# Efficient attention followed by a leaky-ReLU feed-forward layer: one row of q moved from TensorE transposes into a DMA transpose, and three warm-up products left out

## The chip, the cores and the metric

The kernel runs on one core of a Trainium2 chip. The core has five engines with instruction streams of their own: TensorE (PE in the profile; its weight loads are listed as PEld), VectorE (DVE), ScalarE (ACT), GpSimd (POOL) and SyncE (SP), which here only issues DMAs. They share one on-chip memory (SBUF) and one accumulation memory for TensorE (PSUM), and they wait for one another by semaphores. The metric is the device time of one execution in microseconds (us). Lower is better.

## The reference

Inputs are q, k and v of shape (8, 8, 576, 64): batches, heads, positions, head width. The matrices w_in (512 x 2048) and w_out (2048 x 512) follow.

```python
q_s = softmax(q, axis=-1)          # over the 64 of a head
k_s = softmax(k, axis=2)           # over the 576 positions
kv  = einsum('bhsd,bhse->bhde', k_s, v)
x   = einsum('bhsd,bhde->bhse', q_s, kv)      # -> (4608 tokens, 512)
h   = x @ w_in
out = maximum(0.01 * h, h) @ w_out            # (4608, 512), float32
```

Both softmaxes subtract the maximum first and add 1e-9 to the sum.

## The kernel before

**Tiling.** A batch's tensors lie in SBUF as 128 partitions x 4 x 9 x 64 (`HL`, `R`, `D`): a partition holds nine "rows" r of four heads, the other four heads lie in the other 64 partitions. For each batch the kernel forms exp(k), casts v, and multiplies them into kv (`kv`, L333, products of line L325; `kv_pair`, L398, for batch 0). `kd_make` (L341) divides by k's sums. For q it takes the maximum (L229), subtracts it (L288), takes the exponential (`q_exp`, L295), sums (`q_sum`, L302) and multiplies by the reciprocal (`q_norm`, L309). The normalised q has to stand with d on the partitions before TensorE can multiply it with kv. `cross` (L448, products L461) does that product; the result `po` is copied into `xT`, the transposed input of the feed-forward layer.

**How q is transposed.** Batch 0 goes through TensorE: `q_turn_first` (L264) for rows 0 to 3 and `q_transpose` (L425, products L429) for the rest, with a copy from PSUM by `q_keep` (L441, L444 on ScalarE and L446 on VectorE) into the tile `qT`. Batches 2 and later go through a DMA transpose on SP's queue, `q_turn` (L532). Batch 1 goes through three DMA transposes, `turn_next` (L540), from its exponentials `qe` into the tile `X1` (the trace calls it X): seven blocks of 128 columns for the head pair 0 of rows 0 to 6, seven for the head pair 1, and four for rows 7 and 8. `q_cols` (L209) lays batch 1's exponentials out so that each of the three is contiguous.

**Token tiles and order.** The feed-forward layer runs over nine tiles of 512 tokens. A batch has 576, so tile 0 is rows 0 to 7 of batch 0, and tile 1 begins with row 8 of batch 0 and continues with rows 0 to 6 of batch 1. For each tile `layer1` (L547) makes 16 products of the hidden layer, `leaky` (L556, ScalarE) writes them as `gj`, and `layer2` (L568) accumulates the output in PSUM, from which `store` (L560) copies and writes it. Every engine executes its instructions in the order in which the code issues them. The order is written out by hand: `at(t, u, ...)` hangs a step on a point of tile t, and `run(t, u)` issues it there, between products of the layers. In tile 0 the points 32 and later lie between the products of layer 2: at 44.5 comes `kv(1)` and `kd_make(1)`, at 45 `q_transpose(0, 8, 1)` with its copy on ScalarE, and at 46 `attend_next` (L522). This makes the whole xT of tile 1: for each head pair a `cross` of row 8 of batch 0 and one of rows 0 to 6 of batch 1 into the same PSUM banks, and four copies (L530), two on ScalarE and two on VectorE. Four products of layer 2 follow, and then tile 1 begins.

**SP's queue around it.** `next_loads`, at point 32, issues in this order: the first and the second `turn_next`, then the loads of k (batch 2), q's last rows (batch 1), and q and v (batch 2). SP waits at each transpose until the exponentials that it reads are normalised.

**The start.** Before any data is there, TensorE executes idle products of a zero tile: `wake(n, ...)` (L355, products L357) issues one product of n columns for each n; in float32 each is two loads and two products in the trace. `wake(TT, TT, TT, 256)` (L601) comes first, then `wake_on` (L361), a product that waits for the first maxima of q (`nmax`, L238), and shorter idle products between the steps of k's maximum of batch 0 (`k_max_pe` L366, `k_all_dve` L376, `k_all_pe` L380, `k_sub_ps` L390). The w_in matrix comes in eight DMAs from POOL's queue (L126).

**Tiles in memory.** `qe` comes from a pool of two buffers, taken in turn by batches 0, 1, 2 and so on. `X1` is a tile of its own; `qT` of batch 0 and `qX` of batches 2 and later come from a pool of two.

Of the kernel before, what the change touches and what calls it, by code (L numbers as in the profile page):

```python
# [9 lines left out]
BF16 = mybir.dt.bfloat16  # L10
# [9 lines left out]
L = 64  # L20
R = 9
HL = 4
# [3 lines left out]
def kernel(  # L26
# [9 lines left out]
    nc = tc.nc  # L36
# [3 lines left out]
    B, H, S, D = q.shape  # L40
# [6 lines left out]
    P = 128  # L47
    NB = C // P
    NF = F // P
    TT = 512  # L50
# [4 lines left out]
    const_pool = ctx.enter_context(tc.tile_pool(name="const", bufs=1))  # L55
# [4 lines left out]
    qe_pool = ctx.enter_context(tc.tile_pool(name="qe", bufs=2))  # L60
    mx_pool = ctx.enter_context(tc.tile_pool(name="mx", bufs=1))
    small_pool = ctx.enter_context(tc.tile_pool(name="small", bufs=3))
    qT_pool = ctx.enter_context(tc.tile_pool(name="qT", bufs=2))
# [11 lines left out]
    def load(src, b, name, cuts, t=None):  # L75
        t = raw(name) if t is None else t
        flat = src[b].rearrange("h s d -> (h s d)").rearrange(
            "(hl p r d) -> p hl r d", hl=HL, p=P, r=R
        )
        for hs, rs in cuts:  # L80
            nc.sync.dma_start(  # L81
                out=t[:, hs, rs].rearrange("p h r d -> p h (r d)"),
                in_=flat[:, hs, rs].rearrange("p h r d -> p h (r d)"),
            )
        return t

    ALLH, ALLR = slice(0, HL), slice(0, R)
    RA, RB = slice(0, 4), slice(4, R)
    R1, R2, R3 = slice(4, 6), slice(6, 8), slice(8, R)
    R7, RE = slice(0, 7), slice(7, R)  # L90
    st = [{} for _ in range(B)]
# [19 lines left out]
    xT = xT_pool.tile([P, NB, T], BF16)  # L111


    vb2 = [const_pool.tile([P, R, 2, 2, D + 2], BF16, name=f"vb{i}") for i in range(2)]
    kd0 = const_pool.tile([P, 2, 2, 2, D], BF16)
    kd2 = [const_pool.tile([P, 2, 2, D], BF16, name=f"kd{i}") for i in range(2)]
# [92 lines left out]
    def q_cols(b, rs, hs):  # L209
        if b != 1:  # L210
            return st[b]["qe"][:, rs, hs]
        flat = st[b]["qe"].rearrange("p r h d -> p (r h d)")
        cut = R7.stop * 2 * D
        i = 2 if rs.start else hs.start // 2
        return flat[:, i * cut : (i + 1) * cut if i < 2 else R * HL * D].rearrange(
            "p (r h d) -> p r h d", h=hs.stop - hs.start, d=D
        )

    def q_begin(b):
        st[b]["qe"] = qe_pool.tile([P, R, HL, D], BF16, name="qe")  # L220
        if b == 1:
            st[b]["X1"] = const_pool.tile([P, 2 * R, P], BF16, name="X1")
        if b == 0:
            st[b]["qT"] = qT_pool.tile([P, NB, R, L], BF16, name="qT", tag="qT")

    def q_max(b, rs, hs=ALLH):
        n, m = rs.stop - rs.start, hs.stop - hs.start
        st[b]["qmax", rs.start, hs.start] = o = small_pool.tile([P, HL, n], FP32, name="qmax")[:, 0:m]
        nc.vector.tensor_reduce(out=o, in_=st[b]["q"][:, hs, rs], axis=AX.X, op=ALU.max)  # L229
# [76 lines left out]
        st[b]["qrec", rs.start, hs.start] = qrec = small_pool.tile([P, n, HL], FP32, name="qrec")[:, :, 0:m]  # L306
        nc.vector.reciprocal(out=qrec, in_=qsum)

    def q_norm(b, rs, hs=ALLH):  # L309
        n, m = rs.stop - rs.start, hs.stop - hs.start  # L310
        qes = q_cols(b, rs, hs)
        nc.vector.tensor_tensor(  # L312
            out=qes,
            in0=qes,
            in1=st[b]["qrec", rs.start, hs.start].unsqueeze(3).to_broadcast([P, n, m, D]),
            op=ALU.mult,
        )
# [37 lines left out]
    def wake(*cols):  # L355
        for n in cols:
            nc.tensor.matmul(  # L357
                wake_ps[:, 0:n], lhsT=zero, rhs=zero[:, 0:1].to_broadcast([P, n]), start=True, stop=True
            )
# [65 lines left out]
    def q_transpose(b, r0, n, pool=psB_pool, tag=BANK_TAG):  # L425
        ps = pool.tile([P, NB, n, L], BF16, name="psum_qt", tag=tag)
        for rr in range(n):
            for gg in range(2):
                nc.tensor.matmul(  # L429
                    ps[:, gg::2, rr],  # L430
                    lhsT=st[b]["qe"][:, r0 + rr, 2 * gg : 2 * gg + 2].rearrange(
                        "p h d -> p (h d)"
                    ),
                    rhs=ident,
                    is_transpose=True,
                    start=(rr == 0 and gg == 0),
                    stop=(rr == n - 1 and gg == 1),
                )
        st[b]["ps", r0] = ps

    def q_keep(eng, b, r0, n, gs=slice(0, 4)):  # L441
        o, i = st[b]["qT"][:, gs, r0 : r0 + n], st[b]["ps", r0][:, gs]
        if eng is nc.scalar:
            eng.copy(out=o, in_=i)  # L444
        else:
            eng.tensor_copy(out=o, in_=i)  # L446

    def cross(b, gg, outs, rows):  # L448
        for hp in range(2):
            for hh in range(2):  # L450
                half = slice(hp * D, (hp + 1) * D)
                ls = slice(hh * L, (hh + 1) * L)
                if b == 1 and rows.start == R7.stop:
                    rhs = st[b]["X1"][:, 2 * R7.stop :].rearrange("c (r g) l -> c g r l", g=2)[:, gg, :, ls]
                elif b == 1:
                    rhs = st[b]["X1"][:, gg * R7.stop : (gg + 1) * R7.stop, ls]
                elif "qX" in st[b]:
                    rhs = st[b]["qX"].rearrange("c (r g) (h l) -> c g h r l", g=2, h=2)[:, gg, hh, rows]
                else:
                    rhs = st[b]["qT"][:, 2 * hh + gg, rows]  # L460
                nc.tensor.matmul(  # L461
                    outs[hp][hh * D : (hh + 1) * D].rearrange("p (r l) -> p r l", l=L),
                    lhsT=kd0[half, gg, hh, hp] if b == 0 else kd2[b % 2][half, gg, hh],
                    rhs=rhs[half],
                    start=True,
                    stop=True,
                )
# [63 lines left out]

    def q_turn(b, rs=ALLR):  # L532
        if rs.start == 0:
            st[b]["qX"] = qT_pool.tile([P, R * 2, P], BF16, name="qX", tag="qT")
        nc.sync.dma_start_transpose(
            out=st[b]["qX"][:, 2 * rs.start : 2 * rs.stop],
            in_=st[b]["qe"][:, rs].rearrange("p r h d -> p (r h d)"),
        )

    def turn_next(cols, blocks):  # L540
        nc.sync.dma_start_transpose(
            out=st[1]["X1"][:, blocks], in_=st[1]["qe"].rearrange("p r h d -> p (r h d)")[:, cols]
        )

    def layer1(j, ph, c0, n, part=slice(0, 4), first=True, last=True):
# [33 lines left out]
    def at(t, u, *fns):  # L579
        while t > 0 and u >= 32:  # L580
            t, u = t + 1, u - 32
        hooks.setdefault((t, u), []).extend(fns)
# [15 lines left out]


    HA, HB = slice(0, 1), slice(1, 2)  # L600
    wake(TT, TT, TT, 256)  # L601
    nc.gpsimd.tensor_copy(out=gate[:, 0:1], in_=st[0]["k"][:, HL - 1, R - 1, D - 1 : D])
    load_w_in(0)
    k_begin(0)
# [66 lines left out]
        load(v, 1, "v_raw", [(H0, ALLR), (H1, ALLR)], t)  # L671

    def next_loads():
        turn_next(slice(0, 7 * 2 * D), slice(0, 7))
        turn_next(slice(7 * 2 * D, 14 * 2 * D), slice(7, 14))
        st[2]["k"] = load(k, 2, "k_raw", [(H0, ALLR), (H1, ALLR)])
        load(q, 1, "q_raw", [(ALLH, RE)], st[1]["q"])
        st[2]["q"] = load(q, 2, "q_raw", [(ALLH, ALLR)])
        st[2]["v"] = load(v, 2, "v_raw", [(ALLH, ALLR)])
# [11 lines left out]
    at(0, 32, next_loads)  # L691
    at(0, 32, lambda: v_cast(nc.scalar, 1, 1), lambda: k_exp(1, H1))
    at(0, 44.5, lambda: kv(1), lambda: kd_make(1))
    at(0, 45, lambda: q_transpose(0, 8, 1), lambda: q_keep(nc.scalar, 0, 8, 1))
    at(0, 46, attend_next)
    at(1, 8, lambda: q_exp(1, RE))

# [3 lines left out]
    def plan2():  # L701
        b = 2
        at(1, 0, lambda: k_begin(b), lambda: q_begin(b), lambda: k_tree(b, H0), lambda: k_tree(b, H1))
        at(1, 2, lambda: q_max(1, RE), lambda: q_sub(nc.gpsimd, 1, RE))
        at(1, 3, lambda: q_max(b, XR[0]), lambda: q_sub(nc.gpsimd, b, XR[0]))
        at(1, 3, lambda: k_allmax(b), lambda: k_sub(nc.vector, b, H0), lambda: k_sub(nc.vector, b, H1))
        at(1, 6, lambda: q_max(b, XR[1]), lambda: q_sub(nc.gpsimd, b, XR[1]))
        at(1, 13, lambda: q_exp(b, XR[0]), lambda: q_sum(b, XR[0]), lambda: q_norm(b, XR[0]))
        at(1, 13, lambda: v_cast(nc.gpsimd, b, 0), lambda: v_cast(nc.gpsimd, b, 1))
        at(1, 14, lambda: q_sum(1, RE), lambda: q_norm(1, RE))  # L710
        at(1, 15, lambda: k_exp(b, ALLH), lambda: q_turn(b, XR[0]))
        at(1, 15, lambda: turn_next(slice(7 * HL * D, R * HL * D), slice(14, 18)))
        at(1, 16, lambda: q_exp(b, XR[1]), lambda: q_sum(b, XR[1]), lambda: q_norm(b, XR[1]))
        at(1, 17, lambda: q_turn(b, XR[1]))
        at(1, 17, lambda: load_all(4))
        at(1, 23, lambda: kv(b))
        at(1, 24, lambda: kd_make(b))
        at(1, 27, lambda: attend_all(b, (XR[0],)), lambda: attend_all(1, (RE,)))
# [28 lines left out]
    for t in range(3, B - 1):  # L747
        b = t + 1
# [33 lines left out]
    def end_act(j, ph, half):  # L782
# [11 lines left out]
        lambda: q_sub(nc.vector, 0, R3),  # L794
        lambda: q_exp(0, R3),
        lambda: q_sum(0, R3),
        lambda: q_norm(0, R3),
    )
    x1 = (
        lambda: attend(0, (1,), RA),  # L800
# [100 lines left out]
```

## Time and profile before

| | |
|---|---|
| median of 3 runs | 282.1 us (281.68 to 282.16) |
| the profiled execution | 283.07 us |
| its span, first to last instruction | 281.3 us |
| PE busy, share of the span | 272.2 us, 97% |
| DVE, ACT | 159.7 and 159.9 us, 57% each |
| POOL | 49.3 us, 18% |
| q10 and q1 (DMAs issued by engines), q0 (issued by POOL) | 41.9 MB and 4.2 MB |
| q8 and q14 (instructions) | 15 and 7 packets |

The profile is one execution, a little longer than the runs without a profile. A line of a timeline gives the start in us from the span's start, the busy time in us, the engine, the line of the kernel and its operation, what is written and what is read, the shapes and the number of instructions; in brackets stand the idle time of the engine before it and what ended that. "issue" means that nothing the profile shows was waited for. A waits line gives the total, the number and the longest. The chain is followed back from the last instruction to what released each step. In the DMA view a queue has packets, MB, and its share of the time of 16 DMA engines.

### The profile page before, as it was taken

How to read it: one execution, taken by the hardware profiler on the slowest of the kernel's cores; microseconds unless marked ns; L12 is line 12 of the kernel's file. 1: busy time of each engine (PE TensorE's matmuls, PEld its weight loads, DVE VectorE, ACT ScalarE, POOL GpSimd, SP SyncE). 2: the span in 40 equal slices, each digit the busy share in tenths (PEclk: the TensorE clock that was granted, in tenths of full speed). 3: DMA queues.
4: the chain of work that ended last, by engine and by line, in shares of the span. 5: the costliest groups of instructions: out<-in, count | busy, mean ns of one | idle time of the engine just before them, and what ended most of it. 6: DMA issues, size and time to landing. Idle time of an engine off the chain costs nothing.

```text
span 281.3 us, 4853 instructions
## 1 busy us (share of the span) xinstructions
PE 272.2 (97%) x1929; PEld 133.4 (47%) x1956; DVE 159.7 (57%) x227; ACT 159.9 (57%) x283; POOL 49.3 (18%) x54
## 2 busy tenths in 40 slices
PE   8899997999999999999999999999999999999994
PEld 3478644444444454444444544454444444444443
DVE  3986895999999949966885497634610000000011
ACT  4977563685389276755586448643844364146400
POOL 2947380159003002100400050000000000000000
PEclk9999999999999999999999999999999999999999
DMA  7999997999893499089409930333033200330033
GB/s 251 326 209 323 247 235 187 400 320 357 229 396 116 53 329 359 4 223 398 120 0 259 391 90 2 84 77 69 7 86 75 64 11 2 74 75 0 2 75 75
DMA packets 39606, 46.38 MB, mean 165 GB/s; under 512 B 18464, under 2 KB 22816, under 8 KB 39584
## 3 DMA queue, kind: packets, MB, share of 16 engines
q1 hardware_dynamic: 36064, 41.75, 48.9%
q0 software_dynamic: 3360, 4.20, 8.5%
q8 instruction: 15, 0.25, 0.4%
q10 hardware_dynamic: 160, 0.13, 0.2%
q14 instruction: 7, 0.06, 0.1%
HBM read 36.70 MB, written 9.44 MB: 164 GB/s over the span
## 4 chain that ended last, share of the span: by engine, by line
PE 84%; DMA 10%; POOL 2%; issue 1%; ACT 1%; SPq 0%; DVE 0%; ACTq 0%
PE ph L547 41%; PE pout L568 40%; DMA v_raw<-in_v_dram 4%; DMA w_in_sb<-in_moe_w_in_dram 3%; DMA k_raw<-in_k_dram 2%; DMA X<-qe 2%; PE po L461 1%; POOL w_in_sb L126 1%; PE pokv L325 1%; PE pkv L325 1%; SPq L81 0%; ACT gj L556 0%; POOL vb L206 0%; POOL qe L257 0%; ACT ke L194 0%
## 5 line engine op out<-in xcount | busy, mean ns | idle before, releaser
L568 PE MATMUL pout<-w_out_sb,gj 128*128 128x512 bf16 (+2 forms) x574 | 126.4, 373 | 1.2 <-issue 0.3
L547 PE MATMUL ph<-xT,w_in_sb 128*128 128x512 bf16 (+1 forms) x631 | 126.2, 357 | 0.6
L556 ACT ACTIVATE gj<-ph 128x512 bf16<-128x512 f32 x144 | 82.2, 601 | 26.5 <-PE ph L547 25.6
L547 PEld LDWEIGHTS <-w_in_sb 128*128 128x128 bf16 x640 | 62.4, 98 | 62.2 <-DMA w_in_sb<-in_moe_w_in_dram 0.4
L568 PEld LDWEIGHTS <-gj 128*128 128x128 bf16 x592 | 56.5, 98 | 65.3 <-issue 0.2
L562 ACT COPY out_sb<-pout 128x512 f32<-128x512 f32 (+1 forms) x29 | 16.8, 581 | 68.0 <-PE pout L568 40.3
L562 DVE COPY out_sb<-pout 128x512 f32<-128x512 f32 (+1 forms) x8 | 4.8, 636 | 70.8 <-PE pout L568 70.8
L206 POOL CAST vb<-v_raw 128x1152 bf16<-128x1152 f32 x13 | 20.3, 1589 | 84.2 <-DMA v_raw<-in_v_dram 84.2
L305 DVE TENSOR_REDUCE qsum<-qe 128x36 f32<-128x2304 bf16 (+5 forms) x13 | 20.0, 1542 | 10.3 <-ACT qe L296 10.1
L194 ACT ACTIVATE ke<-k_raw 128x1152 bf16<-128x1152 f32 (+2 forms) x12 | 17.8, 1481 | 9.3 <-DVE k_raw L186 9.1
L312 DVE TENSOR_TENSOR qe<-qe,qrec 128x2304 bf16<-128x2304 bf16 (+5 forms) x13 | 22.4, 1726 | 0.4
L229 DVE TENSOR_REDUCE qmax<-q_raw 128x36 f32<-128x2304 f32 (+5 forms) x13 | 20.0, 1537 | 0.8 <-DMA q_raw<-in_q_dram 0.8
L296 ACT ACTIVATE qe<-q_raw 128x2304 bf16<-128x2304 f32 (+5 forms) x13 | 17.1, 1316 | 4.3 <-POOL q_raw L288 3.3
L186 DVE TENSOR_TENSOR k_raw<-k_raw,kall 128x1152 f32<-128x1152 f32 (+1 forms) x9 | 17.3, 1940 | 0.3
L288 POOL TENSOR_TENSOR q_raw<-q_raw,qmax 128x512 f32<-128x512 f32 (+3 forms) x7 | 11.8, 1681 | 21.4 <-DVE qmax L229 19.6
L153 DVE TENSOR_TENSOR t<-t 128x256 f32<-128x256 f32 (+2 forms) x22 | 15.0, 682 | 0.7
L484 ACT CAST xT<-po 128x448 bf16<-128x448 f32 (+3 forms) x34 | 14.4, 516 | 1.1 <-PE po L461 1.1
L288 DVE TENSOR_TENSOR q_raw<-q_raw,qmax 128x2304 f32<-128x2304 f32 (+1 forms) x6 | 13.2, 2202 | 0.3
L345 DVE RECIPROCAL krec<-pokv 128x2 f32<-128x2 f32 x8 | 1.3, 166 | 20.9 <-PE pokv L461 20.9
L153 DVE TENSOR_TENSOR t<-k_raw 128x512 f32<-128x512 f32 (+1 forms) x11 | 12.1, 1103 | 1.3 <-DMA k_raw<-in_k_dram 1.2
L357 PE MATMUL pout<-zero 128*128 128x512 f32 (+3 forms) x18 | 8.9, 616 | 1.0 <-POOL zero L100 1.0
L325 PEld LDWEIGHTS <-ke 64*64 64x64 bf16 x504 | 6.0, 107 | 3.4 <-issue 3.0
(68 smaller groups left out, 106.8 us busy)
## 6 DMA issues: line engine op xcount, KB each, us to landing
out_dram<-out_sb SPq DMA_DIRECT2D x70, 128.0 KB, 2.6
q_raw<-in_q_dram SPq DMA_DIRECT2D x6, 1152.0 KB, 9.3
v_raw<-in_v_dram SPq DMA_DIRECT2D x6, 1152.0 KB, 11.7
k_raw<-in_k_dram SPq DMA_DIRECT2D x5, 1152.0 KB, 6.5
k_raw<-in_k_dram SPq DMA_DIRECT2D x6, 576.0 KB, 6.1
v_raw<-in_v_dram SPq DMA_DIRECT2D x4, 576.0 KB, 7.6
w_in_sb<-in_moe_w_in_dram POOLq DMA_DIRECT2D x8, 256.0 KB, 7.2
w_out_sb<-in_moe_w_out_dram POOLq DMA_DIRECT2D x6, 256.0 KB, 9.4
```

Source lines behind the costliest of these rows:

```text
L153: nc.vector.tensor_tensor(out=o, in0=i0, in1=i1, op=ALU.max)
L186: eng.tensor_tensor(out=ks, in0=ks, in1=st[b]["kall"][:, hs].unsqueeze(2).to_broadcast([P, n, R, D]), op=ALU.subtract,)
L194: nc.scalar.activation(out=st[b]["ke"][:, :, hs].rearrange("p r h d -> p h r d"), in_=st[b]["k"][:, hs], func=AF.Exp,)
L206: eng.tensor_copy(out=o, in_=i)
L229: nc.vector.tensor_reduce(out=o, in_=st[b]["q"][:, hs, rs], axis=AX.X, op=ALU.max)
L288: eng.tensor_tensor(out=qs, in0=qs, in1=st[b]["qmax", rs.start, hs.start].unsqueeze(3).to_broadcast([P, m, n, D]), op=ALU.subtract,)
L305: nc.vector.reduce_sum(out=qsum, in_=q_cols(b, rs, hs), axis=AX.X)
L312: nc.vector.tensor_tensor(out=qes, in0=qes, in1=st[b]["qrec", rs.start, hs.start].unsqueeze(3).to_broadcast([P, n, m, D]), op=ALU.mult,)
L547: nc.tensor.matmul(ph, lhsT=w_in_sb[:, cb, j * P : (j + 1) * P], rhs=xT[:, cb, c0 : c0 + n], start=(cb == 0 and first), stop=(cb == NB - 1 ...
L556: nc.scalar.activation(out=o, in_=ph, func=AF.Prelu, alpha=LEAKY_SLOPE)
L562: copy(out=out_sb, in_=pout)
L568: nc.tensor.matmul(pout, lhsT=g_sb[j // 2][:, j % 2, tsub * P : (tsub + 1) * P], rhs=w_out_sb[:, j, os], start=(j == 0), stop=(j == NF - 1),)
```

## The change

Four things are done.

- Batch 1's exponentials get a tile of their own, `qe1`, of 20 blocks of 128 columns: 0 to 6 head pair 0 of rows 0 to 6, 7 and 8 row 8 of **batch 0**, 9 to 15 head pair 1, 16 to 19 rows 7 and 8 of batch 1. The normalisation of batch 0's row 8 writes its result into blocks 7 and 8.
- The first `turn_next` transposes blocks 0 to 8 in one DMA (nine in place of seven), and `cross` takes row 8 of batch 0 from there. The two TensorE transposes at point 45 and their copy go.
- `X1`, `qT` and `qX` come from one pool of two buffers of 20 blocks; batch 1 no longer takes a buffer of the `qe` pool.
- `wake(TT, TT, TT, 256)` becomes `wake(TT)`.

```diff
+    XH, X8, XE = (slice(0, 7), slice(9, 16)), slice(7, 9), slice(16, 20)
+    qe1 = const_pool.tile([P, XE.stop, P], BF16, name="qe1")
...
     def q_cols(b, rs, hs):
         if b != 1:
             return st[b]["qe"][:, rs, hs]
-        flat = st[b]["qe"].rearrange("p r h d -> p (r h d)")
-        cut = R7.stop * 2 * D
-        i = 2 if rs.start else hs.start // 2
-        return flat[:, i * cut : (i + 1) * cut if i < 2 else R * HL * D].rearrange(
+        blocks = XE if rs.start else XH[hs.start // 2]
+        return qe1[:, blocks].rearrange("p n c -> p (n c)").rearrange(
             "p (r h d) -> p r h d", h=hs.stop - hs.start, d=D
         )
 
+    def turned(name):
+        return qT_pool.tile([P, XE.stop, P], BF16, name=name, tag="qT")
+
     def q_begin(b):
-        st[b]["qe"] = qe_pool.tile([P, R, HL, D], BF16, name="qe")
+        if b != 1:
+            st[b]["qe"] = qe_pool.tile([P, R, HL, D], BF16, name="qe")
+        if b == 0:
+            st[b]["qT"] = turned("qT")[:, 0 : 2 * R].rearrange("p n c -> p (n c)").rearrange(
+                "p (a r l) -> p a r l", r=R, l=L
+            )
         if b == 1:
-            st[b]["X1"] = const_pool.tile([P, 2 * R, P], BF16, name="X1")
-        if b == 0:
-            st[b]["qT"] = qT_pool.tile([P, NB, R, L], BF16, name="qT", tag="qT")
+            st[b]["X1"] = turned("X1")
...
-    def q_norm(b, rs, hs=ALLH):
+    def q_norm(b, rs, hs=ALLH, out=None):
...
-            out=qes,
+            out=qes if out is None else out,
...
-                if b == 1 and rows.start == R7.stop:
-                    rhs = st[b]["X1"][:, 2 * R7.stop :].rearrange("c (r g) l -> c g r l", g=2)[:, gg, :, ls]
+                if b == 0 and rows.start == R3.start:
+                    rhs = st[1]["X1"][:, X8][:, gg : gg + 1, ls]
+                elif b == 1 and rows.start == RE.start:
+                    rhs = st[1]["X1"][:, XE].rearrange("c (r g) l -> c g r l", g=2)[:, gg, :, ls]
                 elif b == 1:
-                    rhs = st[b]["X1"][:, gg * R7.stop : (gg + 1) * R7.stop, ls]
+                    rhs = st[1]["X1"][:, XH[gg], ls]
...
-    def turn_next(cols, blocks):
+    def turn_next(blocks):
         nc.sync.dma_start_transpose(
-            out=st[1]["X1"][:, blocks], in_=st[1]["qe"].rearrange("p r h d -> p (r h d)")[:, cols]
+            out=st[1]["X1"][:, blocks], in_=qe1[:, blocks].rearrange("p n c -> p (n c)")
         )
...
-    wake(TT, TT, TT, 256)
+    wake(TT)
...
-        turn_next(slice(0, 7 * 2 * D), slice(0, 7))
-        turn_next(slice(7 * 2 * D, 14 * 2 * D), slice(7, 14))
+        turn_next(slice(0, X8.stop))
+        turn_next(XH[1])
...
-    at(0, 45, lambda: q_transpose(0, 8, 1), lambda: q_keep(nc.scalar, 0, 8, 1))
...
-        lambda: q_norm(0, R3),
+        lambda: q_norm(
+            0, R3, ALLH, qe1[:, X8].rearrange("p n c -> p (n c)").rearrange("p (r h d) -> p r h d", h=HL, d=D)
+        ),
```

More of the change, by code (lines that the diff above doesn't have):

```diff
@@ L533, in q_turn @@
         if rs.start == 0:
-            st[b]["qX"] = qT_pool.tile([P, R * 2, P], BF16, name="qX", tag="qT")
+            st[b]["qX"] = turned("qX")[:, 0 : 2 * R]
         nc.sync.dma_start_transpose(
@@ L711, in plan2 @@
         at(1, 15, lambda: k_exp(b, ALLH), lambda: q_turn(b, XR[0]))
-        at(1, 15, lambda: turn_next(slice(7 * HL * D, R * HL * D), slice(14, 18)))
+        at(1, 15, lambda: turn_next(XE))
         at(1, 16, lambda: q_exp(b, XR[1]), lambda: q_sum(b, XR[1]), lambda: q_norm(b, XR[1]))
```

## The prediction

> **What bounds the kernel now.** I read the page's busy times first, then the list of waits of TensorE (PE), then the chain that ended last, and then the timeline around the two places that the change touches.
>
> ```profile
> PE 272.2 (97%) x1929; PEld 133.4 (47%) x1956; DVE 159.7 (57%) x227; ACT 159.9 (57%) x283; POOL 49.3 (18%) x54
> ```
>
> PE is busy for 97% of the span, so a gain has to come out of its remaining idle time or out of its work. The waits of PE (total us, times, longest) name the idle time:
>
> ```profile
> PE po L461 <- DMA X<-qe: 1.2, 1, 1.2
> PE pout L357 <- POOL zero L100: 1.0, 1, 1.0
> PE kallp L383 <- DVE kr L378: 0.6, 2, 0.3
> ```
>
> The longest is a wait of 1.2 us for the transposed q of batch 1. The chain, in order of time, has the same place on it, followed by PE work almost without a break to the end:
>
> ```profile
> 42.36 4.30 DMA X<-qe
> 46.66 0.04 issue
> 46.70 0.38 PE po L461 x4
> 47.08 0.97 PE pout L568 x4
> ```
>
> So whatever moves the end of this transfer, or PE's arrival at it, moves the end of the kernel, and after 47 us nothing but PE's own work counts. PE's timeline there:
>
> ```profile
> 42.71 0.86 PE L325 MATMUL pkv<-vb,ke 64*64 64x65 bf16 x72
> 43.72 0.38 PE L568 MATMUL pout<-w_out_sb,gj 128*128 128x512 bf16 x1 [0.16 <-issue]
> 43.94 0.28 PE L429 MATMUL psum_qt<-ident,qe 128*128 128x128 bf16 x2
> 44.05 1.03 PE L568 MATMUL pout<-w_out_sb,gj 128*128 128x512 bf16 x4
> 45.01 0.22 PE L461 MATMUL po<-qT,kd 64*64 64x64 bf16 x4
> 45.06 0.36 PE L461 MATMUL po<-X,kd 64*64 64x448 bf16 x4
> 45.25 0.20 PE L461 MATMUL po<-qT,kd 64*64 64x64 bf16 x4
> 46.70 0.38 PE L461 MATMUL po<-X,kd 64*64 64x448 bf16 x4 [1.25 <-DMA X<-qe]
> ```
>
> The first transfer (head pair 0) is in time: its products start at 45.06 without a wait. Only the last four products, which read the second transfer (head pair 1), wait, from 45.45 to 46.70.
>
> **Why is the second transfer late?** It is issued at 42.36 and moves as much as the first. In the trace's DMA records its packets run from 43.5 to 44.5, and 15 of its 16 engines have landed by 44.97. The sixteenth lands at 46.66. The DMA view of 44.4 to 45.5 us shows what else moved:
>
> ```profile
> q1 hardware_dynamic: 51, 0.04, 54.1%
> q8 instruction: 1, 0.02, 6.2%
> ```
>
> One packet of q8, a fetch of 16 KB of instructions, held one of the 16 engines (6.2% of them) for the whole stretch. Its record starts at 44.47 and takes 1.09 us; the last two small packets of the transfer, on one engine, follow at 45.54. Q8 fetches 15 times (page: 0.25 MB) while PE issues 1929 + 1956 recorded instructions, about 259 for each fetch, so I take it to be PE's own code. The same shape is at 19.80: such a fetch, and then one of 16 engines lands w_in's third late part at 22.17 where the others had it by 21.19. The fetch at 44.47 came within 0.1 us of missing the transfer.
>
> **The change, part by part.** The sum is made against the profiled execution: 283.07 us, of which the span is 281.3 and 1.8 lie around it. The median of the runs shown is 282.1, 1.0 below it; I carry differences over.
>
> 1. *Row 8 of batch 0 leaves PE.* Two transposes of 128 columns (L429) and their loads go. The L568 products start at 43.727 and 44.054 around them, 0.327 apart, against 0.216 without them (44.054, 44.270): PE gets 0.11 us back. The scalar copy (L444, 0.37 at 44.25) goes too, but ScalarE then waits 0.83 for PE, so it is worth nothing. With the wait still there PE would only wait 0.11 longer.
>
> 2. *The first transfer has nine blocks.* The 18-block transfer issued at 147.13 has its packets from 148.35 to 150.67: 0.13 us a block, as the second one (7 blocks in 0.9). Two blocks more are 0.26 us: it lands at about 43.7 in place of 43.45, and its readers come at 44.9, so 1.2 us cover it. SP's issue grows by about 0.1 (1.22 to 1.33 for 7 blocks, 1.90 to 2.05 for 18), and SP is idle then until DVE ends the second half at 42.29. The first transfer's packets end at 43.0, with the two blocks at 43.25, and the second one's begin at 43.5: 0.25 remain. Without that cover the second transfer would be pushed by up to 0.26. The normalisation of row 8 (L312, 0.43 at 24.80) writes another tile, same shape: nothing; SP's wait for it ended 14 us earlier.
>
> 3. *Own buffers.* Batch 1's exponentials leave the rotating pool, so batch 2 takes the second buffer and batch 3 the first; both are written (from 60 us on) long after their former readers. The transposed q of batches 0 and 1 take the two qT buffers; batch 2's transposes (66.68) follow batch 0's last reader (21.68), batch 3's (94.7) follow the last product on X (73.5). Nothing.
>
> 4. *Three idle products fewer.* The row of L357 before 6.6 us has 8 products for four calls: a call is two products and two loads. So 12 instructions go, and PE is idle from about 2.7 until nmax is there at 6.03. wake_on then starts at 6.07 in place of 6.58, which frees nothing, as kmax is only ready at 7.96. What may be lost is the clock:
>
> ```profile
> 4.57 0.34 PEld L357 LDWEIGHTS pout<-zero 128*128 128x128 f32 x1 [0.52 <-issue]
> 5.42 0.34 PEld L357 LDWEIGHTS pout<-zero 128*128 128x128 f32 x1 [0.52 <-issue]
> 6.06 0.19 PEld L357 LDWEIGHTS pout<-zero 128*128 128x128 f32 x1 [0.30 <-issue]
> ```
>
> Loads of 0.34 become 0.19, and products that started every 0.85 take 0.43 each (L362: two in 1.02): PE runs at half speed for its first 4.8 us of unbroken work, and the records have the full clock from 5.8 on. After the change work begins anew at 6.07. The same 4.8 us from there open the clock at 10.9. If the two products of 1.0 to 2.7 still count, it opens at 9.2; if the gaps after 7.8 have to be made up (about 2 us), at 12.9. Until then the products between 8.1 and 12.1 (0.30, 0.39, 0.44, 0.70, 0.33, 0.39, 0.44, 0.91) stream 20 passes of 128 columns, 0.107 each at full clock, so at most 2.1 us more. Gaps of 0.3, 0.3 and 0.2 and DVE's own order swallow about half. Followed through kT, kr, kallp and the subtractions on DVE, the first kv product (12.24) comes 0 late if the clock opens at 9.2, 0.4 late at 10.9, and 0.85 to 1.0 late at 12.9. PE works on without pause to 22.09 and there waits 0.1 for w_in (22.17): so D, PE's lateness at 22.2, is between 0 and 1.0, and I take 0.3, for the one duration that the trace shows. From there to 45 us PE has no wait to absorb it; DVE's chain to the second transfer hangs on loads and POOL, ScalarE is 2.0 early for it, so it doesn't shift with D.
>
> [...]
>
> 5. *Code moves.* Twelve instructions fewer ahead of the kv products put the fetch 12 instructions later in PE's stream. Of the 15 fetches those that follow a burst of small products start some 1.2 us after it (an estimate from where they stand in PE's stream), which puts the crossing near the end of the 144 loads and products of 42.7 to 43.4; 12 more there are 0.06 to 0.1 us, and up to 0.5 if they reach beyond it. With D the fetch starts at 44.9 (44.55 to 45.9). The transfer's last engine is through at 44.52. So it is no longer held, lands at 44.97, and PE, which would reach it at 45.34 + D, doesn't wait. Next in line is then PE alone: the copies to xT (0.59, 0.69) follow the products and are covered by four L568 products (1.04).
>
> Sum: -1.25 (wait) - 0.11 (transposes) + 0.3 (D) = -1.06: 282.0 for a profiled execution, 281.0 for the median; I say **281.1**. The bounds: D = 0 gives 280.7; a fetch that still catches the transfer leaves a wait until 46.7, and the change is worth 0 up to D = 1.36.
>
> **Rivals.**
>
> *The wait stays* (282.1, chance 0.30). Either the fetch still falls within the transfer, or the runs without the profiler never had the held engine: they are 1.0 us shorter, which speaks for that. Then only -0.11 + D is left, 281.9 to 282.6. For the forecast speaks that the miss was so narrow; the same narrowness speaks for a coin-flip from run to run. [...]
>
> *Slower: the clock opens too late* (283.4, chance 0.18). If the work from 6.07 on is not dense enough and the clock opens only around 16 (twice 4.8 us), the products from 12.24 to 16.4 (0.70, 0.40, 0.86, 0.65, 0.70, 0.40, 1.04) run at half speed as well: about 2 us on top of 1.0, D = 3. It decides from D = 1.36 on, where the old wait is used up; minus that, +1.6 at D = 3, and half of it for an opening around 14: 282.9 to 283.7, in the middle 283.4. For it: the gaps after 8.1. Against it: cold products fill the gaps better.
>
> *The two blocks push the second transfer* (281.3, chance 0.05): by 0.26, of which 0.37 of slack swallow all but what D changes; its sum is within the forecast's.
>
> **Numbers.** Forecast 0.47 (281.1, own range 280.6 to 281.5), wait stays 0.30, slower 0.18, pushed 0.05. Range 280.5 to 283.1. A measurement of this kernel can tell 0.2% (0.56 us) from no change: faster 0.49, same 0.32, slower 0.19.
>
> **What would show it.** Loads of 0.34 after 6.1 and the time where they become 0.19; the start of L403 (12.24) and of the L547 products at 22.21, whose shift is D; X's three landings; the q8 packet after 44.5; no row "PE po <- DMA X" above 0.2, and L568 after the last X product at about 45.9 in place of 47.02. A q8 packet before 44.5 with a landing near 46.7 proves the first rival; L403 after 13.3 proves the second. I would be wrong altogether if DVE's chain moved the issue at 42.36.

## The result and the profile after

The changed kernel took 283.18 us in the median of 17 runs, the kernel before beside it 281.97 in 17: a ratio of 1.0035 (95% interval 1.002 to 1.005; the medians alone give 1.0043), slower where the forecast was 281.1. Over all measurements, with 41 runs of the changed kernel and 135 of the kernel before beside it and beside the experiments, the medians are 283.2 and 281.8.

And yet the profiled execution of the changed kernel took 282.21 us with a span of 280.4, 0.9 less than the profiled one before, nearly the 282.0 of the prediction's sum. Both executions were untypical (34 of the 135 runs before are above 282.5, and 13 of the 41 after are below it), and that is the lesson of this case. (Lines of code lie 6 to 8 further on: L363 is `wake`, L368 `wake_on`, L469 `cross`, L555 and L576 the two layers.) The waits of PE:

```profile
PE pout L368 <- DVE nmax L244: 3.1, 1, 3.1
PE pout L363 <- POOL zero L100: 1.0, 1, 1.0
PE pout L576 <- issue: 0.3, 2, 0.2
```

The wait of 1.25 us on X is gone, as forecast. In its place PE waits 3.1 us for the first maxima of q, where there had been idle products. The timeline of PE at 45 us:

```profile
44.12 1.24 PE L576 MATMUL pout<-w_out_sb,gj 128*128 128x512 bf16 x5 [0.16 <-issue]
45.29 0.64 PE L469 MATMUL po<-X,kd 64*64 64x64 bf16 x16
45.86 1.04 PE L576 MATMUL pout<-w_out_sb,gj 128*128 128x512 bf16 x4
46.73 3.62 PE L555 MATMUL ph<-xT,w_in_sb 128*128 128x512 bf16 x16
```

The 16 products run without a break: row 8's come from X too, and both transfers have landed, at 43.42 and 44.45. Tile 1 begins at 46.73 in place of 47.89. Of the start, the weight loads:

```profile
6.13 0.09 PEld L368 LDWEIGHTS pout<-zero,nmax 128*4 128x4 f32 x2 [4.64 <-DVE nmax L244]
...
10.20 0.23 PEld L374 LDWEIGHTS kT<-identf,kmax 128*128 128x128 f32 x1
10.63 0.55 PEld L363 LDWEIGHTS pout<-zero 128*128 128x128 f32 x2 [0.20 <-issue]
11.43 0.30 PEld L389 LDWEIGHTS kallp<-identf,kr 128*64 128x64 f32 x4 [0.25 <-DVE kr L384]
11.92 0.30 PEld L363 LDWEIGHTS pout<-zero 128*128 128x128 f32 x2 [0.20 <-issue]
```

Two loads of the zero tile take 0.55 us at 10.63, and 0.30 at 11.92, as they did at full clock before. The trace's clock records give full speed from 11.7, against 5.8. The first kv product of batch 0 starts at 12.88 (before 12.24) and the third part of layer 1's products at 22.66 (22.21): PE is 0.45 late.

### The profile page after: what moved, and what is told of

It is laid out like the page before. It is cut to its first block, busy times and chain, and to the rows that moved or that the text cites. A ratio compares the mean times of both kernels' runs of the same rounds, so it can differ in the third digit from the quotient of the medians.

```text
span 280.4 us, 4836 instructions
## 1 busy us (share of the span) xinstructions
PE 270.7 (97%) x1921; PEld 132.2 (47%) x1948; DVE 158.7 (57%) x227; ACT 159.3 (57%) x282; POOL 49.8 (18%) x54
## 4 chain that ended last, share of the span: by engine, by line
PE 85%; DVE 8%; DMA 4%; issue 1%; ACT 0%; SPq 0%; DVEq 0%; ACTq 0%
PE pout L576 40%; PE ph L555 39%; DMA qX<-qe 2%; DMA k_raw<-in_k_dram 2%; PE po L469 2%; DVE t L155 2%; DVE qmax L235 1%; DVE k_raw L188 1%; PE pout L363 1%; PE pokv L331 1%; DVE out_sb L570 1%; DVE qe L318 1%; DVE qsum L311 1%; PE pkv L331 1%; PE pkv L409 0%
## 5 line engine op out<-in xcount | busy, mean ns | idle before, releaser
L576 PE MATMUL pout<-w_out_sb,gj 128*128 128x512 bf16 (+2 forms) x574 | 126.3, 373 | 1.2 <-issue 0.3
L555 PE MATMUL ph<-xT,w_in_sb 128*128 128x512 bf16 (+1 forms) x631 | 126.1, 357 | 0.5
L555 PEld LDWEIGHTS <-w_in_sb 128*128 128x128 bf16 x640 | 62.3, 98 | 62.1 <-DMA w_in_sb<-in_moe_w_in_dram 0.2
L576 PEld LDWEIGHTS <-gj 128*128 128x128 bf16 x592 | 56.6, 98 | 65.5 <-issue 0.2
L294 POOL TENSOR_TENSOR q_raw<-q_raw,qmax 128x512 f32<-128x512 f32 (+3 forms) x7 | 11.8, 1684 | 20.3 <-DVE qmax L235 18.1
L492 ACT CAST xT<-po 128x448 bf16<-128x448 f32 (+3 forms) x34 | 14.4, 515 | 1.1 <-PE po L469 1.1
L155 DVE TENSOR_TENSOR t<-t 128x256 f32<-128x256 f32 (+2 forms) x22 | 13.2, 598 | 0.7
L363 PE MATMUL pout<-zero 128*128 128x128 f32 (+3 forms) x12 | 6.3, 624 | 1.0 <-POOL zero L100 1.0
## 6 DMA issues: line engine op xcount, KB each, us to landing
v_raw<-in_v_dram SPq DMA_DIRECT2D x6, 1152.0 KB, 11.7
```

Of the source, the lines that this page charges most:

```text
L155: nc.vector.tensor_tensor(out=o, in0=i0, in1=i1, op=ALU.max)
L294: eng.tensor_tensor(out=qs, in0=qs, in1=st[b]["qmax", rs.start, hs.start].unsqueeze(3).to_broadcast([P, m, n, D]), op=ALU.subtract,)
L555: nc.tensor.matmul(ph, lhsT=w_in_sb[:, cb, j * P : (j + 1) * P], rhs=xT[:, cb, c0 : c0 + n], start=(cb == 0 and first), stop=(cb == NB - 1 ...
L576: nc.tensor.matmul(pout, lhsT=g_sb[j // 2][:, j % 2, tsub * P : (tsub + 1) * P], rhs=w_out_sb[:, j, os], start=(j == 0), stop=(j == NF - 1),)
```

## The experiments

Theory A: the missing idle products let the clock open late, and PE carries the lateness to the end. Theory B: the nine-block transfer and the buffers cost the time. Theory C: the 12 missing PE instructions move the fetches of code onto something that then waits. Some kernels take one part alone, the others more or less of the suspected cost.

**The late clock alone** (three times)

```diff
-    wake(TT, TT, TT, 256)
+    wake(TT)
```

> The kernel before with wake(TT) in place of wake(TT, TT, TT, 256), nothing else. Theory A (the clock opens later and PE carries the lateness to the end): about the changed kernel's time, 282.8 to 283.4 us against 282.0, a ratio of 1.003 to 1.005, with loads of 0.34 us or half-speed products after 6.1 us. Theory B (the nine-block transfer and the new buffers cost the time): 282.0, ratio 1.000.

Measured: 282.05 us (12 runs), ratio 1.0016 (0.9987 to 1.0045). Neither A nor B is decided: the times fell into two groups, so it was run again.

> The kernel before with wake(TT) alone once more, since its first 12 times fell in two groups (7 near 281.8, 5 from 283.0 to 284.9). Theory A (the late clock alone costs the time): median 282.8 to 283.4. Rival (the late clock costs only together with the nine-block transfer): median 282.0, with at least half of the times under 282.3.

Measured: 283.06, ratio 1.0034 (1.0017 to 1.0051). Third:

> The kernel before with wake(TT) alone, a third time. Theory A: mean 282.6 to 283.2 us, ratio 1.003 to 1.005.

Measured: 283.98 (8 runs, mean 283.76, above the range), ratio 1.0055 (1.0028 to 1.0083). The three means are 0.33, 0.87 and 1.72 us above the kernel before beside them; together, 32 runs, it is 0.88 (standard error 0.19). A holds.

**The rest alone** (twice): the changed kernel with `wake(TT, TT, TT, 256)`.

> The changed kernel with the three idle products put back, so the nine-block transfer, the removed TensorE transposes and the buffers alone. Theory A: 281.7 to 282.0, ratio 0.999 to 1.000 (0.11 us of transposes saved, and now and then a wait for the held engine). Theory B: 283.0, ratio 1.004.

Measured: 281.94, ratio 0.9987 (0.9964 to 1.0011).

> The changed kernel with the three idle products put back, once more, to narrow its interval. Theory A (only the late clock costs): 281.5 to 282.0 us, ratio 0.998 to 1.000. Theory B (the nine-block transfer and the buffers cost something as well): above 1.001.

Measured: 281.56, ratio 0.9996 (0.9979 to 1.0013). The mean of both is 0.22 below the kernel before (standard error 0.13), which agrees with the 0.11 of the transposes and nothing for the transfer and the buffers; B falls.

**As many instructions, no filling**: the changed kernel with

```diff
-    wake(TT)
+    wake(TT, 16, 16, 16)
```

> The changed kernel with wake(TT, 16, 16, 16): as many PE instructions at the start as before, so the fetches of code lie in PE's stream where they lay, but PE is nearly idle from 3 to 6 us. Theory A (clock): 282.8 to 283.4, ratio 1.003 to 1.005, as the changed kernel. Theory C (the 12 missing instructions move the fetches of code onto something that then waits): 282.0, ratio 1.000.

Measured: 283.60, ratio 1.0038 (1.0009 to 1.0068). With as many loads and products as before, three pairs of them of 16 columns, the clock opened at 13.4 us; with those of 512, 512 and 256 columns in their place (the rest alone) at 6.7 and 4.4. C's reading, that the missing instructions themselves cost, falls.

**As few instructions, an early clock** (meant so): the changed kernel with

```diff
-    wake(TT)
+    wake(TT, TT, TT, 256)
...
     k_max_pe(0, 0)
-    wake(P)
...
     k_max_pe(0, 1)
-    wake(P)
...
     q_turn_first(0, 0)
-    wake(384)
```

> The changed kernel with the three first idle products put back and three later ones left out in their place (the two of 128 columns and the second of 384), so that as many PE instructions are missing before the kv products of batch 1 as in the changed kernel, but the clock opens at 6 us. Theory A (clock): 281.5 to 282.0, ratio 0.997 to 1.000. Theory C (the 12 missing instructions move fetches of code onto something that waits): 283.2, ratio 1.004.

Measured: 283.47 (281.39 to 286.51), ratio 1.0026 (1.0005 to 1.0048) without the two longest. This looks like C, but the profile shows that the experiment missed its aim. Its busy times in stretches of 3.4 us (sum and count of PE, PEld, DVE, ACT and POOL, then the granted clock):

```profile
8.40:11.80 3.40, 2.28 (x13) 1.26 (x14) 3.33 (x10) 3.40 (x19) 3.40 (x7) 1.00 1.07 395
11.80:15.20 3.40, 2.88 (x25) 1.37 (x23) 2.40 (x8) 2.81 (x4) 2.97 (x5) 0.50 1.12 207
15.20:18.60 3.40, 3.37 (x33) 2.35 (x33) 2.81 (x8) 1.69 (x4) 1.06 (x2) 0.50 1.13 210
18.60:22.00 3.40, 3.40 (x35) 2.79 (x34) 2.62 (x6) 1.70 (x5) 2.06 (x4) 0.99 1.12 223
```

The clock, open since 5.0, closed at 11.8 and came back at 18.6: PE reached layer 1's third part at 24.43, 2.2 late. The kernel before, with its two products of 128 columns, was busy for 2.77 in place of 2.28 us in the same stretch (its second profiled execution, below) and kept the clock:

```profile
8.40:11.80 3.40, 2.77 (x17) 1.66 (x18) 3.33 (x11) 3.33 (x19) 3.40 (x7) 1.00 1.08 394
```

What closed it is not shown by one stretch alone: the one ahead (4.98 to 8.40) was busy for 2.28 us too and didn't close the clock, nor did one of 2.14 (7.72 to 11.14) in that execution of the kernel before. In this kernel two such stretches follow each other.

The granted share of the clock, which is on record for every execution, settles C all the same. (Time before the first opening is not in it: the changed kernel's profiled execution has 1.000.) The 6.83 us that this trace has at half speed (0.50 above) take about 0.012 off it, and half of that time about 0.006, an estimate from a span of 282. Six of the twelve executions have 0.987 to 0.993 and took 283.5 to 286.5 us. The other six have 0.998 or 1.000, so the clock stayed open; they took 281.4 to 283.5, on the mean 282.2 (standard error 0.3), beside 281.9 for the kernel before. Where the clock stays open, the missing instructions cost nothing that can be told from the noise. C's 283.2 falls, and A is borne out once more.

**Less filling**: the changed kernel without the idle products of 128, 256, 128 and 384 columns between the steps of k's maximum.

> The changed kernel without the idle products of 128, 256, 128 and 384 columns between the steps of k's maximum as well, so that PE is less dense from 8 to 12 us: more of the suspected cost. Theory A: the clock opens only at 15 to 20 us, PE is 2 to 3 us late at 22 and the time is 284 to 286 us, ratio 1.008 to 1.014. If the lateness of the clock is not what costs, 282 to 283.

Measured: 283.82 (6 runs), ratio 1.0062 (1.0039 to 1.0086). Full clock at 16.9; layer 1's third part at 23.59. The direction is A's; the lateness is 1.4 in place of 2 to 3, and without idle products in its way the first kv product starts almost on time, at 12.40.

**Two idle products put back**: the changed kernel with `wake(TT, TT, TT)`.

> The changed kernel with two of the three idle products put back: wake(TT, TT, TT), PE busy from 1.0 to about 6.0 us. Theory A: the clock opens before 8 us, no late start of the kv products, 281.4 to 281.9 us, ratio 0.997 to 1.000; a candidate for a version faster than both. If the clock opens after 10 us in spite of it, 283.

Measured: 281.76, ratio 1.0007 (0.9986 to 1.0027). Full clock at 6.9, no late kv product. A's time, but not faster than before. Its profile reaches tile 1 at 45.88, 0.76 earlier than the better trace of the kernel before, and ends no earlier: it then waits 0.6 us for the transposes of batch 2.

**And without the later idle product of 384 columns**

> As the one with wake(TT, TT, TT), and without the idle product of 384 columns after the first kv products: eight PE instructions fewer than with all three idle products, at an early clock. If the fetch of code is what holds an engine of the second transpose, the fetch then starts after it has landed (45 us or later), no profile shows a wait of PE on X, and times above 282.6 are rare: median 281.5, ratio 0.997. If the clock closes again in the gap (as it did without three of the later idle products), 283 and more.

Measured: 282.03 (281.52 to 285.26), ratio 1.0034 (1.0004 to 1.0064). The profile (282.30) shows the fetch at 46.4 and the second transfer landed at 44.88 on all engines, as expected; but 4 of 12 runs took 283.6 to 285.3, which was not. No trace of those was taken. The two longest have a granted clock of 0.994, as the estimate above gives for half of the 6.83 us; the other two have 1.000 and 0.999, and what made them long is open.

**The same kernels again.** The kernel before:

> The kernel before, unchanged, for a second profiled execution and as a measure of the noise: ratio 1.000. Its times so far lie in two groups, 281.2 to 282.2 us and 282.6 to 283.8. If the held engine makes the upper group, a profile from the lower group has the second transpose landing on all 16 engines together and no wait of PE on X; one from the upper group has a landing 1 to 2 us late on one engine.

Measured: 281.99, ratio 1.0014 (0.9999 to 1.0029). Its profiled execution took 281.96 us, a typical one, and this is what it looks like at 45 us:

```profile
45.20 0.22 PE L461 MATMUL po<-qT,kd 64*64 64x64 bf16 x4
45.25 0.36 PE L461 MATMUL po<-X,kd 64*64 64x448 bf16 x4
45.44 0.20 PE L461 MATMUL po<-qT,kd 64*64 64x64 bf16 x4
45.47 0.36 PE L461 MATMUL po<-X,kd 64*64 64x448 bf16 x4
45.77 1.04 PE L568 MATMUL pout<-w_out_sb,gj 128*128 128x512 bf16 x4
46.64 0.59 PE L547 MATMUL ph<-xT,w_in_sb 128*128 128x512 bf16 x2
```

There is no wait on X. The second transfer lands whole at 44.45; the fetch of code starts at 44.42, after its packets. Tile 1 begins at 46.64, and the changed kernel's at 46.73 or later. The changed kernel again:

> The changed kernel again, for a second profiled execution and times beside the others. Theory A: 282.9 to 283.3, spread over 2 us, ratio 1.004; in the profile the lateness of the L555 products at 22.2 us follows the time at which products reach full speed: about 0.45 us if that is at 11.7 as in the first profile, 1.0 to 1.6 us if it is at 13 or later.

Measured: 283.49, ratio 1.0047 (1.0021 to 1.0072); its profiled execution took 284.04 us. Full clock only at 14.1, PE 1.3 late at 23.53, as expected. But there was more; its waits:

```profile
PE pout L368 <- DVE nmax L244: 2.9, 1, 2.9
PE pkv L331 <- ACT ke L196: 1.2, 1, 1.2
```

and its ScalarE around it:

```profile
39.37 1.14 ACT L206 CAST vb<-v_raw 128x1152 bf16<-128x1152 f32 x1
43.48 1.15 ACT L206 CAST vb<-v_raw 128x1152 bf16<-128x1152 f32 x1 [2.97 <-DMA v_raw<-in_v_dram]
44.53 1.16 ACT L196 ACTIVATE ke<-k_raw 128x1152 bf16<-128x1152 f32 x1
```

The load of batch 1's v is released by ScalarE between two of tile 0's `gj` (L678 here, `more_loads`). With a late PE it is issued at 31.42 in place of 30.10 and lands at 43.45 in place of 40.54; the kv products of batch 1, 1.3 late themselves, wait 1.25 more. A cost that the prediction did not have. The late issue alone does not make it, since PE is late by as much: the load's second half also took 11.6 us from issue to landing in place of 10.0. The three executions with this wait have 10.8 to 11.6 there. Two that issue it about as late or later have 9.9 and no wait (the late clock alone, first time, and the kernel with as few instructions). Why the load sometimes takes longer is open. The third time:

> The changed kernel a third time, beside the late clock alone. If the parts add up: its mean lies within 0.4 us of the wake-only kernel's of the same call, or below. If the nine-block transfer costs with a late clock: 0.7 us or more above, with PE waiting for the first transpose in the profile.

Measured: 282.29, ratio 1.0013 (0.9988 to 1.0038), and 283.98 for the late clock alone beside it: the changed kernel wasn't above it. (In the first pair of measurements its mean was 0.8 us above, standard error about 0.4.) Over the 41 runs it is 0.88 us above the kernel before (standard error 0.14), just what the late clock alone costs (0.88); with the rest's -0.22 the parts would give 0.66, which is within the noise.

**v earlier**: the changed kernel with

```diff
-    at(0, 27, more_loads)
+    at(0, 23, more_loads)
```

> The changed kernel with batch 1's v loaded four steps earlier (at point 23 in place of 27). If part of the cost comes through the late load of v: no wait of the kv products on ScalarE in the profile, mean 282.5 to 282.9, about 0.5 us below the changed kernel beside it. If not, or if v then only takes bandwidth from q: as the changed kernel, 283.0 to 283.5, or above.

Measured: 282.64, ratio 1.0030 (1.0006 to 1.0054). In its profile the clock opened at 13.75 and PE was 1.2 late at 23.41, but no kv product waited, and the time was 282.54. This is one execution, and the late clock alone, first time, 1.26 late, had no such wait with v in its old place, so the trace doesn't prove that the earlier load took the wait away. The times don't prove a gain either: the changed kernel beside it had 282.29.

All profiled executions in one table, in us; "full clock" is from the trace's clock records, "layer 1" the start of its third part's products, "wait" the longest of PE between 40 and 48 us, from 0.2 us on: X is the second transfer, ke the exponentials of k, which ScalarE makes after it has cast v.

| kernel | full clock | first kv | layer 1 | wait | time |
|---|---|---|---|---|---|
| before | 5.8 | 12.24 | 22.21 | X 1.25 | 283.07 |
| before, again | 4.3 | 12.51 | 22.31 | none | 281.96 |
| changed | 11.7 | 12.88 | 22.66 | none | 282.21 |
| changed, again | 14.1 | 13.44 | 23.53 | ke 1.25 | 284.04 |
| changed, third | 11.5 | 12.89 | 22.67 | none | 282.52 |
| late clock alone | 13.7 | 13.69 | 23.47 | X 1.1 | 283.96 |
| late clock alone, second | 9.7 | 12.31 | 22.24 | none | 281.62 |
| late clock alone, third | 14.4 | 13.59 | 23.73 | ke 0.75 | 283.88 |
| rest alone | 6.7 | 12.14 | 22.10 | X 1.6 | 283.02 |
| rest alone, second | 4.4 | 12.25 | 22.43 | none | 281.56 |
| short filling | 13.4 | 13.46 | 23.24 | ke 0.5 | 283.02 |
| v early | 13.75 | 13.54 | 23.41 | none | 282.54 |
| as few instructions | 5.0, closed 11.8 to 18.6 | 12.82 | 24.43 | none | 283.57 |
| less filling | 16.9 | 12.40 | 23.59 | none | 284.19 |
| two products put back | 6.9 | 12.02 | 21.81 | none | 281.97 |
| and without 384 columns | 5.9 | 12.28 | 22.40 | none | 282.30 |

An execution with a clock open by 9.7 that stays open, and no wait, takes 281.6 to 282.3. From 281.8, the lateness of layer 1 against 22.21 and the wait, added up, give each time of the table within 0.5 but two: for the changed kernel again 281.8 + 1.3 + 1.25 = 284.35, where 284.04 was measured. Less filling and two products put back took 1.0 and 0.6 longer than the sum; there PE waited once more at 74 and 72 us, for 1.2 and 0.6 us.

## Why the prediction was wrong, point by point

**What bounds the kernel.** That PE's own time and its lateness at 45 us set the end held in 12 of the 16 profiled executions; in the other four PE waited once more at 72 to 74 us, for 0.2 to 1.2 us. The wait on X was read rightly in the one execution shown: it was a held engine, and in the three traces that have it (before, late clock alone, rest alone) a fetch of code starts 2.1 to 2.5 us after the second transfer's issue, and one engine lands 1.6 to 1.7 later than the other 15. In the traces without it the fetch mostly starts 2.6 us or more after the issue. Two, with `wake(TT, TT, TT)` and with less filling, have it 2.4 and 2.5 after and no held engine, so what decides within that overlap stays open.

**Step 5, the sum's -1.25: failed.** It was taken off the median as if every execution had the wait. The typical execution has none (281.96 us, X landed at 44.45): of 135 runs of the kernel before, 34 are above 282.5. The sign was on the page: the profiled execution was 1.0 above the median of the others, about the size of the wait. The prediction had this as its first rival, with 0.30, and gave -0.11 + D for it. For the two executions first profiled the sum does come out: 283.07 - 1.25 - 0.11 + 0.45 = 282.16, where 282.21 was measured. The step also put the fetch of code at 44.9 (44.55 to 45.9); in the changed kernel's three traces it starts at 46.5 to 49.7. So the transfer was not held, as forecast, but the place of the crossing was read wrongly; why it lies so much later stays open.

**Step 4, D: mis-sized.** The mechanism was right, from the load of 0.34 us to the late first kv product; the 0.3 was not. It rested on one duration (4.8 us until the clock opened). In seven of the eight profiled executions that start with `wake(TT)` or `wake(TT, 16, 16, 16)` and keep the later idle products, the clock opened after 11.4, in five of them after 13, and D was 0.45 to 1.5; the wake-only runs average +0.88. With that mean for D, the first rival's -0.11 + D gives +0.77, where +0.88 (standard error 0.14) was measured. The rival's own 281.9 to 282.6 left out what step 4 allowed: with D = 1.0 it is 283.0. Openings at 13.4 to 14.4 made D 1.0 to 1.5; step 4 ended at 12.9 and 1.0, and the slower rival's half for an opening around 14 (+0.8 after a wait of 1.36) means a D near 2.2. In three executions the wait for v added 0.5 to 1.25 on top.

**"It doesn't shift with D", of the chain to the second transfer: failed.** The second transfer is issued between 41.55 and 42.36 us in the nine executions whose layer 1 is at most 0.5 late, and between 42.28 and 43.50 in the seven that are 1.0 late or more. ScalarE's copy that releases the load of v shifts as well (29.91 before, 31.22 in the changed kernel again). The prediction took a shift of the issue at 42.36 for the sign of being wrong altogether; the kernel before, unchanged, already has it at 41.85 in its second trace, so the sign can't decide.

**Steps 1 to 3: right in what they cost.** The rest alone gives -0.22 (standard error 0.13), with 0.11 forecast. The first transfer with nine blocks landed 5.3 us after its issue at 38.12, but at 43.42, before its readers at 45.29; in the traces of the changed kernel no product waited for it. The cover of 0.25 us between the two transfers, in step 2, was not there: with nine blocks the second transfer, or its 15 free engines, lands 2.9 to 3.0 us after its issue in every trace, with seven 2.6 to 2.7. So the third rival's push of 0.26 happened; in the changed kernel it cost nothing that shows, because the landing at 44.45 still came ahead of the readers.

**The slower rival** named the right mechanism and the right sign with 0.18. Its point from which it decides, D = 1.36, used up a wait that typical executions don't have; without it any D above 0.1 costs. Its sign, a first kv product after 13.3, came in five of the eight executions with a pause. That its 283.4 lies near the measured 283.18 is luck: neither its D of 3 nor the wait of 1.36 that it takes off stands in a trace of the changed kernel.

No version was clearly faster than both kernels: the rest alone comes nearest (0.9987 and 0.9996, both intervals reach over 1).

## What to carry to other kernels

Before a wait in a profile is counted as a gain, compare the profiled execution's time with the median: when it is longer by about that wait, the wait may be its accident, and the typical execution has nothing to give there. Idle products that look like waste can pay for the clock of what follows: here leaving out the last of the four cost nothing that could be told from the noise (+0.3 us, standard error 0.25), and leaving out three cost 0.9 on the mean. A late engine also delays the loads that another engine releases on its progress (here that of v, issued at 31.42 in place of 30.10), so look for those before calling a chain independent.

## What the runs showed of the hardware

PE's clock opened at 4.3 to 6.9 us in the seven profiled executions that were busy with products of 256 and 512 columns from 1.0 us on without a pause of note, and at 9.7 to 14.4 in the eight with a pause of 1.8 us or more before 6 us and the later products in place. The periods of full clock in the traces (276.48, 273.07, 269.65 and 266.24 us) differ by 3.41 or multiples of it, and the closed stretch of 6.83 us is two of them. When it opens, PE's busy time does not tell: in three executions PE was busy for 3.25, 3.29 and 3.32 of the 3.41 us right before the opening (late clock alone, second; changed, third; before, again), while in four others (changed, again; late clock alone, first and third; short filling) it had been busy for 3.26 to 3.28 of 3.41 us and the clock opened only 3.41 us after that. The ends of products are modelled in the profile, so what decides stays open. And the clock closed after two stretches of 3.4 us in a row that were busy for 2.28 and 2.29 us (as few instructions); single ones of 2.14 (before, again) and 2.15 (without 384 columns) didn't close it.

A fetch of 16 KB of instructions held one DMA engine for 0.9 to 1.1 us and delayed the landing of an unrelated transpose by 1.6 to 1.7 us in the three traces that show it. No wait of PE listed for these traces names a fetch; what was delayed in three of them is the transfer on the same engine.
